# Softmax in halves of eight consecutive blocks, one early transfer of even V rows, and unchained loads of wo

## The chip, the core and the metric

The kernel runs on one core of one Trainium2 chip. The core has a matrix engine (PE, with its weight loads shown as PEld), a vector engine (DVE), a scalar engine (ACT), a general engine (POOL) and a queue engine (SP), each with its own list of instructions and synchronised by semaphores. DMA transfers are issued from SP, ACT and POOL. The metric is the device time of one execution in microseconds (us), lower is better.

## What is computed

Two branches read the same normalised input xn of 2048 tokens by 512: a dilated sliding-window attention with 32 heads of 16 (A), and a gated MLP whose gate mixes all tokens (B). The result is x + A + B.

```python
def _A_ref(x, wqkv, wo):
    H = 32
    Dh = D // H
    W, dil = (8, 2)
    qkv = (lambda x, *d: x.transpose(*d))((x @ wqkv).reshape(B, S, 3, H, Dh), 2, 0, 3, 1, 4)
    q, k, v = (qkv[0], qkv[1], qkv[2])
    idx = pos[:, None] - off[None, :]
    mask = idx >= 0
...
    logits = jnp.einsum('bhsd,bhswd->bhsw', q, kg) * scale
    logits = jnp.where(mask[None, None, :, :], logits, -1000000000.0)
    attn = _softmax(logits, axis=-1)
    o = jnp.einsum('bhsw,bhswd->bhsd', attn, vg)
    return (lambda x, *d: x.transpose(*d))(o, 0, 2, 1, 3).reshape(B, S, D) @ wo

def _B_ref(x, w_in, w_sp, b_sp, w_out):
    z = _gelu(jnp.einsum('bsd,df->bsf', x, w_in))
    z1 = z[..., :Fh].copy()
    z2 = _layernorm(z[..., Fh:], axis=-1)
    g = jnp.einsum('ts,bsf->btf', w_sp, z2) + b_sp[None, :, None]
    return jnp.einsum('bsf,fd->bsd', z1 * g, w_out)
```

Each token attends to itself and to the tokens 2, 4, ... 14 before it.

## The kernel before

The program builds a list of named tasks. A task is one instruction, one DMA, or a short run of matmuls; it belongs to one engine and has the buffers that it reads and writes. From these the program works out what each task must wait for, and an order written out for every engine (ORDERS, L206) says in which sequence each engine works through its tasks. An engine works its list strictly in order: where one task waits, those behind it wait too. Estimates given to the tasks (`est`) make no instruction.

The tokens are in 16 blocks of 128, and the work goes through these stages, each named by the prefix of its tasks:

- **ldx, bnst, norm, xTr / xTd**: x is loaded, normalised and transposed (the first four blocks on PE, the others by transposing DMAs on SP).
- **Q, K, V, z2, z1** on PE: projections by 512 or 448 columns. Their results lie in six banks of PSUM, used as three pairs in turn (0-1, 2-3, 4-5), and ACT empties them: QKe, halo and Ve (L677 to L683, L652), z2g and z1g with the gelu (L818), z2s (L826) with the sum of squares. A pair may be written again once ACT has emptied it. z1_7_0 is the first half of the columns of block 7, z1g7 its gelu.
- **Vw** on SP (L657) writes V to a scratch array in DRAM. **ldV** (L983, issued on ACT) reads it back, so that a partition holds rows two tokens apart: ldV0_k has rows of the even tokens, ldV1_k of the odd ones. The 15 slots of the even rows are read by the even blocks; the odd rows take slots 15 to 22, where the logits stood before, and then slots that the even blocks no longer need.
- **prod, padd** on DVE and **lg** on PE (L694, L698, L707) form the logits of four blocks, **lge** on ACT (L745) copies them to the staging buffer. When all four groups are there, four transposing DMAs **lgT0 to lgT3** on SP (L756) bring tokens to partitions: each holds four consecutive blocks.
- **softmax** (L761 to L796), twice: a tree of three maxima (sm1 to sm3), subtraction (ssub), exponential on ACT (sexp, L783), a tree of three sums (sz1 to sz3), 1/sum as exp(-ln) on ACT (sln L787, srec L789), and the multiplication (sattn, L794). Before, one half is the even blocks and the other the odd blocks, so that the first half needs all four transposes.
- **zn** (L851 on ACT for blocks 12 to 15, L855 on DVE for the others) normalises z2. **T1 to T4** (DVE) are sums of z2 blocks.
- **wT** on SP (L892) loads and transposes w_sp for a pair of output blocks, **S13, S2, S4** (L902 to L908, DVE) sum quarters of it. **P1 to P7** (L930, PE) are seven products of eight matmuls each, which take the place of eight (a Strassen scheme) for each of eight pairs of blocks: (0,2), (4,6), (8,10), (12,14), (15,13), (11,9), (7,5), (3,1). Their banks alternate between 0 to 2 and 3 to 5. fk copies the first product to another bank, S5, S2e, Sc and S3e evacuate (L936, ACT), h adds (L953, DVE), g11, g12, g21 and g22 finish the gate, u multiplies by z1 (L962, L968), and a transposing DMA uT (L972, SP) turns it.
- **pv, pva, pvc** (L1000 to L1008, DVE): attention times V for a pair of blocks, **OTd** its transpose on SP (L1012).
- **out** (PE): four matmuls with wo (L1037) and seven with w_out (L1041), on banks 6 and 7, where **os** (L1032) has put the residual from **ldxr**. **fin** (L1050) evacuates, **st** stores.

wo comes in four loads on POOL's queue (ldwo0 to ldwo3, L1117) that share one channel, so each waits until the one before it has landed; w_out (ldwout) is issued among them. All wait for the last z1 product, whose weights lie in the same memory.

An even V load before the change waits for all V writes and for the four logit transposes; ACT's order has ldV1_7 ahead of z1g3.

Of the kernel before, what the change touches and what calls it, by code (L numbers as in the profile page):

```python
# [14 lines left out]
class Plan:  # L15
# [191 lines left out]
    pe="""  # L207
warm xTr0 fill0 z2_0_0 xTr1 z2_0_1 z2_1_0 xTr2 z2_1_1 xTr3 z2_2_0 z2_2_1 z2_3_0 z2_3_1 Q0_0 K0_0 Q0_1 Q0_2 K0_2
K0_1 K0_3 V2 V1 V0 Q0_3 V7 V3 V4 V6 V5 Q1_0 K1_0 K1_1 Q1_2 Q1_1 Q1_3 K1_3 z2_4_1 K1_2 z2_6_1 z2_6_0 z2_4_0
z2_5_0 z2_5_1 lg0_0 z2_7_1 z2_7_0 V10 V8 V11 V9 K2_0 Q2_0 K2_2 Q2_1 K2_1 Q2_2 K2_3 Q2_3 z2_8_1 z2_8_0 z2_9_0  # L210
z2_9_1 z2_10_1 z2_10_0 z2_11_0 V13 z2_11_1 V14 lg1_0 V12 V15 K3_1 K3_0 Q3_0 K3_2 Q3_1 Q3_3 Q3_2 z2_12_0 z2_12_1
K3_3 z2_13_1 z2_13_0 z2_14_1 z2_15_1 z2_14_0 lg2_0 z2_15_0 z1_0_0 z1_2_1 z1_0_1 z1_2_0 z1_4_0 z1_6_0 z1_4_1
z1_6_1 z1_8_0 z1_8_1 z1_10_1 z1_10_0 z1_12_1 z1_12_0 z1_14_0 z1_14_1 lg3_0 z1_15_1 z1_15_0 z1_13_1 z1_13_0
z1_9_1 z1_9_0 z1_7_1 z1_7_0 z1_11_1 z1_11_0 z1_3_1 z1_3_0 z1_1_0 z1_1_1 z1_5_1 P1_0 z1_5_0 P5_0 P2_0 P1_1 P6_0
P3_0 P7_0 P2_1 P6_1 P5_1 P4_0 P7_1 P3_1 P1_2 P4_1 P2_2 P5_2 P6_2 P1_3 P7_2 P2_3 P4_2 out0_0 P3_2 P6_3 P5_3 P1_4
P3_3 P7_3 out2_0 P5_4 out4_0 P4_3 P6_4 P2_4 P7_4 P1_5 P4_4 P3_4 out6_0 out8_0 P5_5 out10_0 P6_5 P2_5 P1_6 P7_5
out12_0 P4_5 P3_5 P5_6 P6_6 out14_0 P3_6 P7_6 P2_6 P4_6 P1_7 out15_0 P5_7 P6_7 out13_0 out11_0 P2_7 P7_7 P3_7
P4_7 out9_0 out7_0 out5_0 out3_0 out1_0 out1_1
""".split(),
    act="""  # L220
actprime ldw_in2a_1 ldw_in2b_1 ldx3 xTe0 xTe1 z2g0 xTe2 xTe3 z2g1 z2s0 z2g2 z2g3 halo0_0 QKe0_0 QKe0_2 halo0_1
QKe0_1 Ve2 halo0_2 Ve1 Ve0 QKe0_3 Ve3 halo0_3 Ve5 Ve6 Ve4 QKe1_0 halo1_1 z2s1 halo1_0 QKe1_1 Ve7 QKe1_3 halo1_3
z2s2 QKe1_2 z2s3 halo1_2 z2g4 z2g6 z2g5 zm0 z2g7 z2s4 Ve8 Ve11 Ve10 Ve9 halo2_0 z2s5 QKe2_0 z2s6 halo2_2 QKe2_1
lge0 halo2_1 QKe2_2 QKe2_3 halo2_3 z2s7 z2g8 z2g9 z2g10 z2s8 z2g11 Ve14 Ve13 lge1 Ve15 zm1 Ve12 z2s9 QKe3_0
z2s10 QKe3_1 QKe3_2 z2g12 QKe3_3 z2s11 z2g13 z2s12 z2g14 zm2 z2s13 z2g15 z1g0 z2s14 z1g2 z2s15 z1g4 z1g6 lge2
z1g8 z1g10 z1g12 lge3 z1g14 z1g15 z1g13 zn13 z1g9 zn12 z1g7 ldxr0 z1g11 bspf ldV1_7 z1g3 zn14 zn15 z1g1 fk_0
ldV0_0 z1g5 sexp0 fk_1 S5_0 S2e_0 sln0 Sc_0 srec0 S3e_0 S2e_1 S5_1 g11_0 g11_1 S3e_1 g12_0 g21_0 fk_2 Sc_1
ldV0_9 ldxr2 g22_0 g21_1 sexp1 S2e_2 g22_1 S5_2 fk_3 ldV0_11 os0_0 g11_2 S3e_2 g21_2 os2_0 g12_1 Sc_2 ldxr8
S2e_3 g22_2 ldxr6 S5_3 ldxr4 g12_2 fin0_0 g11_3 os4_0 S3e_3 fk_4 sln1 Sc_3 st0_0 ldV0_13 srec1 ldxr10 fin2_0
S2e_4 os6_0 S5_4 fin4_0 ldxr12 os8_0 S3e_4 g22_3 ldV1_6 st2_0 ldV1_4 g12_3 g21_4 Sc_4 g21_3 st4_0 fk_5 fin6_0  # L230
g11_4 os10_0 fin8_0 ldV1_2 os12_0 S2e_5 g22_4 S5_5 ldV1_0 ldxr14 S3e_5 g11_5 st6_0 fin10_0 fk_6 ldxr15 g12_4
fin12_0 st10_0 os14_0 Sc_5 st8_0 ldxr13 ldxr11 g22_5 S5_6 g12_5 g21_5 S2e_6 fin14_0 os15_0 Sc_6 st12_0 S3e_6
st14_0 ldxr9 g11_6 g22_6 g12_6 os13_0 g21_6 fin15_0 fk_7 ldxr7 S5_7 os11_0 fin13_0 fin11_0 S2e_7 os9_0 st11_0
ldxr5 ldxr3 S3e_7 st15_0 os7_0 Sc_7 g11_7 st13_0 ldxr1 g12_7 g22_7 g21_7 fin9_0 os5_0 st9_0 fin7_0 st7_0 os1_1
os3_0 fin5_0 st5_0 os1_0 fin3_0 st3_0 fin1_0 st1_1
""".split(),
    dve="""
zeros steps0 steps1 bnst0 bnag0 norm0 bnst1 bnag1 xTf0 norm1 bnst2 bnag2 bnst3 bnag3 norm2 bnst5 bnag5 norm3
bnst7 bnag7 bnst8 bnst6 bnag6 bnst4 bnag8 norm7 bnag4 bnst9 bnst10 norm5 bnst11 norm6 norm4 bnag11 bnag9 bnag10
prod0_0 prod0_2 prod0_1 norm8 padd0_1 bnst12 bnst13 padd0_2 prod0_3 norm11 bnst15 norm10 bnag15 bnag13 norm9  # L240
bnag12 bnst14 padd0_3 bnag14 prod1_0 prod1_1 zq0 norm13 prod1_2 norm12 zq1 padd1_1 norm14 norm15 padd1_2 prod1_3
prod2_1 padd1_3 prod2_0 zv0 zv1 padd2_1 prod2_2 prod2_3 padd2_2 zq2 smask padd2_3 prod3_1 prod3_0 zv2 prod3_2
padd3_1 zq3 prod3_3 zv3 padd3_2 padd3_3 zn3 zn5 zn0 zn2 S13_1 zn11 zn1 S13_0 zm3 zn6 zn10 zn8 zn9 zn7 T1_0 zn4
T1_1 sm1_0 T3_0 S2_0 S2_1 sm2_0 sm3_0 T3_1 ssub0 T2_1 S4_0 T2_0 T4_1 sz1_0 sz2_0 sz3_0 sm1_1 T4_0 sm2_1 S4_1
sm3_1 ssub1 sattn0 h_0 pv0 pv2 pva2048_0 pva1024_0 pvc0 S13_2 S2_2 u_0 S4_2 sz1_1 h_1 pv4 sz2_1 S13_3 pv6 S2_3
pva2048_1 sz3_1 S4_3 u_4 h_2 pva1024_1 pvc1 pv8 pv10 S13_4 pva2048_2 u_8 h_3 pva1024_2 S2_4 pvc2 S4_4 sattn1
pv12 pv14 pva2048_3 pva1024_3 S13_5 pvc3 u_12 S2_5 pv13 h_4 pv15 S13_6 S4_5 pva2048_4 pva1024_4 S2_6 pvc4 pv9
S4_6 pv11 h_5 pva2048_5 u_11 pva1024_5 u_15 pvc5 pv5 S13_7 h_6 pv7 S2_7 pva2048_6 u_7 pva1024_6 pvc6 S4_7 pv3
pv1 pva2048_7 pva1024_7 pvc7 h_7 u_3 u_1 fin1_1
""".split(),  # L250
# [4 lines left out]
    sp="""
ldx0 ldx1 ldw_in2a_0 ldw_in2b_0 ldx2 ldx4 ldx5 ldx8 ldx6 ldx7 ldq ldk ldx9 ldx10 ldx11 ldwv xTd7 xTd5 xTd4 ldx15
xTd6 ldx12 ldx14 Vw1 Vw2 ldx13 Vw0 xTd8 Vw3 Vw7 xTd11 xTd10 Vw4 Vw6 Vw5 xTd9 xTd12 xTd13 xTd14 xTd15 Vw9 Vw10
Vw11 Vw8 wT1_1 ldw_in1 wT0_0 wT0_1 Vw15 Vw12 Vw14 wT1_0 Vw13 lgT0 lgT1 lgT3 lgT2 wT2_0 wT2_1 wT3_0 wT3_1 OTd0
uT_0 wT4_0 uT_2 wT4_1 OTd1 uT_4 uT_6 wT5_0 uT_8 uT_10 OTd2 wT5_1 wT6_0 wT6_1 uT_12 OTd3 uT_14 OTd4 wT7_0 wT7_1
uT_15 uT_13 uT_11 uT_9 OTd5 uT_7 OTd6 uT_5 OTd7 uT_3 uT_1 st1_0  # L260
# [926 lines left out]
```

## Time and profile before

| | us |
|---|---|
| median of 3 runs (lowest, highest) | 228.18 (227.88, 228.59) |
| the profiled execution: its own time | 228.81 |
| its span, first to last instruction | 227.1 |
| busy PE / DVE / ACT / POOL | 221.8 / 203.8 / 147.8 / 35.3 |
| the first and the last product P on PE start | 100.15 / 211.2 |
| the last matmul ends | 224.8 |

The page's chain that ended last gives 85% of the span to PE, by line:

```profile
PE 85%; DMA 6%; SPq 3%; ACT 2%; DVE 2%; issue 1%; ACTq 0%; DVEq 0%
PE ps L930 33%; PE ps L807 15%; PE ps L669 12%; PE ps L1041 11%; PE ps L646 6%; PE ps L1037 6%; DMA arena<-in_B_w_sp_dram 3%; DMA arena<-in_A_x_dram 2%; SPq L756 2%; DMA arena<-arena 1%; ACT arena L818 1%; PE ps L707 1%; ACT arena L851 1%; DVE fpool L595 1%; DVE arena L902 1%
```

The V loads in the table of DMA issues (line, count, size, us from issue to landing):

```profile
arena<-vscr ACTq DMA_DIRECT2D x6, 256.0 KB, 4.2
arena<-vscr ACTq DMA_DIRECT2D x1, 1152.0 KB, 7.7
arena<-vscr ACTq DMA_DIRECT2D x1, 1024.0 KB, 6.0
```

How to read it: a row of the timeline has the start, the length, the engine, the line, the operation and the count of instructions that follow each other, and in brackets the idle time before with what ended it. Matmul lengths are modelled and longer than the distance from one to the next, so PE is timed by starts. A span's share of idle time costs only on the engine that sets the end.

### The profile page before, as it was taken

How to read it: one execution, taken by the hardware profiler on the slowest of the kernel's cores; microseconds unless marked ns; L12 is line 12 of the kernel's file. 1: busy time of each engine (PE TensorE's matmuls, PEld its weight loads, DVE VectorE, ACT ScalarE, POOL GpSimd, SP SyncE). 2: the span in 40 equal slices, each digit the busy share in tenths (PEclk: the TensorE clock that was granted, in tenths of full speed). 3: DMA queues.
4: the chain of work that ended last, by engine and by line, in shares of the span. 5: the costliest groups of instructions: out<-in, count | busy, mean ns of one | idle time of the engine just before them, and what ended most of it. 6: DMA issues, size and time to landing. Idle time of an engine off the chain costs nothing.

```text
span 227.1 us, 3070 instructions
## 1 busy us (share of the span) xinstructions
PE 221.8 (98%) x1130; PEld 115.6 (51%) x1142; DVE 203.8 (90%) x208; ACT 147.8 (65%) x258; POOL 35.3 (16%) x40
## 2 busy tenths in 40 slices
...
PEclk9999999999999999999999999999999999999999
DMA  6969605148982000959749995887996495936562
GB/s 191 298 157 186 190 0 146 22 92 214 225 219 61 0 0 4 160 146 309 124 140 217 266 202 120 171 210 141 280 169 152 115 203 140 213 67 151 128 124 69
DMA packets 84767, 34.18 MB, mean 151 GB/s; under 512 B 69280, under 2 KB 84400, under 8 KB 84752
## 3 DMA queue, kind: packets, MB, share of 16 engines
...
## 4 chain that ended last, share of the span: by engine, by line
PE 85%; DMA 6%; SPq 3%; ACT 2%; DVE 2%; issue 1%; ACTq 0%; DVEq 0%
PE ps L930 33%; PE ps L807 15%; PE ps L669 12%; PE ps L1041 11%; PE ps L646 6%; PE ps L1037 6%; DMA arena<-in_B_w_sp_dram 3%; DMA arena<-in_A_x_dram 2%; SPq L756 2%; DMA arena<-arena 1%; ACT arena L818 1%; PE ps L707 1%; ACT arena L851 1%; DVE fpool L595 1%; DVE arena L902 1%
## 5 line engine op out<-in xcount | busy, mean ns | idle before, releaser
L930 PE MATMUL ps<-arena 128*128 128x448 bf16 x448 | 86.7, 352 | 0.8 <-ACT arena L818 0.4
L930 PEld LDWEIGHTS ps<-arena 128*128 128x128 bf16 x448 | 43.6, 98 | 42.9 <-ACT arena L818 0.8
L807 PE MATMUL ps<-arena 128*128 128x448 bf16 x256 | 51.3, 355 | 0.2 <-DVE arena L629 0.2
L807 PEld LDWEIGHTS ps<-arena 128*128 128x128 bf16 x256 | 30.5, 121 | 19.1 <-issue 1.3
L1000 DVE TENSOR_TENSOR arena<-arena 128x4096 bf16<-128x4096 bf16 x16 | 36.2, 2285 | 0.3
L936 ACT ACTIVATE arena<-ps 128x448 bf16<-128x448 f32 x32 | 17.3, 540 | 29.4 <-PE ps L930 25.3
L694 DVE TENSOR_TENSOR arena<-arena 128x4096 bf16<-128x4096 bf16 x16 | 36.0, 2283 | 0.2 <-PE ps L707 0.2
L818 ACT ACTIVATE arena<-ps 128x896 bf16<-128x896 f32 x32 | 28.9, 916 | 6.2 <-PE ps L807 6.2
L669 PE MATMUL ps<-arena 128*128 128x512 bf16 x126 | 28.5, 379 | 0.1
L1004 DVE TENSOR_TENSOR arena<-arena 128x4096 bf16<-128x4096 bf16 (+1 forms) x16 | 28.1, 1753 | 0.2
L698 DVE TENSOR_TENSOR arena<-arena 128x4096 bf16<-128x4096 bf16 x12 | 27.4, 2282 | 0.0
L1041 PE MATMUL ps<-arena 128*128 128x512 bf16 (+2 forms) x117 | 26.9, 366 | 0.1
L600 POOL TENSOR_TENSOR fpool<-fpool 128x1 f32<-128x1 f32 x16 | 19.2, 1207 | 20.0 <-DVE fpool L598 19.9
L669 PEld LDWEIGHTS ps<-arena 128*128 128x128 bf16 x128 | 14.5, 113 | 13.1
L677 ACT ACTIVATE arena<-ps 128x1024 bf16<-128x1024 f32 x16 | 16.2, 1025 | 4.0 <-PE ps L669 4.0
L1050 ACT ACTIVATE arena<-ps 128x512 bf16<-128x512 f32 (+1 forms) x16 | 9.4, 589 | 13.4 <-PE ps L1041 13.4
L1041 PEld LDWEIGHTS ps<-arena 128*128 128x128 bf16 x119 | 11.4, 98 | 12.8
L1037 PE MATMUL ps<-arena 128*128 128x512 bf16 (+2 forms) x63 | 15.5, 365 | 0.3
L826 ACT ACTIVATE arena<-arena 128x896 bf16<-128x896 bf16 x16 | 15.2, 950 | 0.0
L646 PE MATMUL ps<-arena 128*128 128x512 bf16 x61 | 14.3, 379 | 0.2
L595 DVE BATCH_NORM_STATS2 fpool<-arena 128x6 f32<-128x512 bf16 x16 | 10.6, 676 | 3.2 <-DMA arena<-in_A_x_dram 3.1
L958 ACT ACTIVATE arena<-arena,fpool 128x448 bf16<-128x448 bf16 x16 | 10.4, 662 | 4.1 <-DVE arena L953 2.4
...
## 6 DMA issues: line engine op xcount, KB each, us to landing
...
arena<-vscr ACTq DMA_DIRECT2D x6, 256.0 KB, 4.2
arena<-vscr ACTq DMA_DIRECT2D x1, 1152.0 KB, 7.7
arena<-vscr ACTq DMA_DIRECT2D x1, 1024.0 KB, 6.0
```

The source lines that it names most:

```text
L600: T("pool", lambda g: g.tensor_tensor(Fv("rstd", 1, b), Fv("mv", 1, 2 * b + 1), Fv("mhalf", 1), ALU.pow), reads=[("mv", b), "mhalf"], writ ...
L646: last = t.matmul(bank(k + i), AC(off["xnT"] + dc * S + 128 * (b + i), [[1, 128]]), AC(off["wv_raw"] + 512 * dc, [[1, 512]]), start=(dc == ...
L669: last = t.matmul(bank(k + which), AC(off["wqk"] + 1024 * dc + col0, [[4, 128]]), AC(off["xnT"] + dc * S + 512 * j, [[1, 512]]), start=(dc ...
L694: T("dve", lambda v: v.tensor_tensor(pbv, qb, kb, ALU.mult), reads=[("QT", c, j), ("KT", c, j), ("KTpad", c, j)], writes=[("pb", s_)], est ...
L698: T("dve", lambda v: v.tensor_tensor(A("pb", 4096, 4096 * a), A("pb", 4096, 4096 * a), A("pb", 4096, 4096 * b), ALU.add), reads=[("pb", b) ...
L807: last = t.matmul(bank(k + hf, HF), AC(off["xnT"] + dc * S + t0, [[ts, 128]]), AC(off["w_in"] + 1792 * dc + c0, [[1, HF]]), start=(dc == 0 ...
L818: T("act", lambda a: a.activation(A(nm, FH, FH * b).rearrange("p (t n) -> p t n", t=2), PC(512 * k, [[512, 2], [1, HF]]), ACTF.Gelu_apprx_ ...
L930: last = t.matmul(bank(k, HF), AC(lo + 128 * s, [[1, 128]]), mov(s), start=(first and s == 0), stop=(s == 7), skip_group_check=True)
L1000: T("dve", (lambda iv, tv, av: lambda v: v.tensor_tensor(tv, iv, av, ALU.mult))(iv, tv, av), reads=[("attn", pairs[i][b]) for b in blks] + ...
L1004: T("dve", (lambda n: lambda v: v.tensor_tensor(AC(off["Vs"], [[4096, 2], [1, n]]), AC(off["Vs"], [[4096, 2], [1, n]]), AC(off["Vs"] + n, ...
L1037: t.matmul(po, AC(off["OT"] + 512 * os_ + 128 * cc, [[1, 128]]), AC(off["wo"] + 512 * cc + c0, [[1, n]]), start=False, stop=False, skip_gr ...
L1041: last = t.matmul(po, AC(off["uT"] + FH * us + 128 * fc, [[1, 128]]), AC(off["w_out"] + 512 * fc + c0, [[1, n]]), start=False, stop=(fc == ...
```

## The change

Softmax works on blocks 0 to 7 and 8 to 15 in place of even and odd blocks. All 15 slots of even V rows come in one transfer, which waits for the V writes alone and is created ahead of the logit transposes; these now wait for it. The loads of wo have a channel each. Two estimates differ. All five orders are new; the main stages keep their sequence, and inside them tasks change places. The core of the diff:

```diff
-                T("pe", mm, reads=[("pb", s_), "mlog"], writes=[("ps", 6), ("ps", 7)], est=570.0,
+                T("pe", mm, reads=[("pb", s_), "mlog"], writes=[("ps", 6), ("ps", 7)], est=760.0,
...
+        def ld_v(par, k0, n):
+            s0 = k0 + 8 * par
+            src = bass.AP(tensor=vscr.tensor, offset=vscr.offset + (par + 2 * k0 + 2) * 512,
+                          ap=[[16 * 512, 128], [1024, n], [1, 512]])
+            dma("act", lambda e: e.dma_start(AC(off["Ve"] + 512 * s0, [[512, n], [1, 512]]), src), 128 * 512 * 2 * n,
+                ("Ve", s0), reads=[("vscr", i) for i in range(-1, NB)] + ([("lgTd", i) for i in range(4)] if par else []), writes=[("Ve", s0 + i) for i in range(n)],
+                name="ldV%d_%d" % (par, k0), prio=LOW)
...
-                    128 * 1024 * 2, ("lgT", n), reads=["stage"] + [("lgs", j) for j in range(NJ)],
+                    128 * 1024 * 2, ("lgT", n), reads=["stage"] + [("lgs", j) for j in range(NJ)] + [("Ve", 0)],
...
-        def softmax(par):
+        def softmax(half):
...
-            a0 = off["attn"] + 256 * par
-            ks = [("attn", b) for b in range(par, NB, 2)]
-            nm = "%d" % par
+            a0 = off["attn"] + 2048 * half
+            ks = [("attn", b) for b in range(8 * half, 8 * half + 8)]
+            nm = "%d" % half
...
-                T("dve", lambda v: v.tensor_tensor(AC(off["Za"], [[128, 8], [1, 128]]), AC(a0, [[512, 8], [1, 128]]),
-                                                   AC(a0 + 128, [[512, 8], [1, 128]]), op),
+                T("dve", lambda v: v.tensor_tensor(AC(off["Za"], [[128, 8], [1, 128]]), AC(a0, [[256, 8], [1, 128]]),
+                                                   AC(a0 + 128, [[256, 8], [1, 128]]), op),
...
-            dv = AC(a0, [[512, 8], [32, 8], [1, 32]])
+            dv = AC(a0, [[256, 8], [32, 8], [1, 32]])
...
-            ev = AC(a0, [[512, 8], [1, 256]])
+            ev = AC(a0, [[256, 8], [1, 256]])
...
-                      reads=[("m2", j), ("rstd2", j)], writes=[("z2", b, 0), ("z2", b, 1)], est=c_act(FH), name="zn%d" % b)
+                      reads=[("m2", j), ("rstd2", j)], writes=[("z2", b, 0), ("z2", b, 1)], est=c_act(FH) + 210.0, name="zn%d" % b)
...
             if j == NJ - 1:
+                ld_v(0, 0, 15)
                 lg_transposes()
...
-                128 * 512 * 2, "wo", writes=[("wo", c)], name="ldwo%d" % c)
+                128 * 512 * 2, ("wo", c), writes=[("wo", c)], name="ldwo%d" % c)
...
-        vloads = {0: [(0, 0, 9)], 1: [(0, 9, 2)], 2: [(0, 11, 2)], 3: [(0, 13, 2)], 4: [(1, 7, 8), (1, 6, 1)],
+        vloads = {4: [(1, 7, 8), (1, 6, 1)],
                   5: [(1, 4, 2)], 6: [(1, 2, 2)], 7: [(1, 0, 2)]}
```

The new orders, where the prediction follows them (the ones before stand in the kernel above):

```diff
     pe="""
...
+z1_8_1 z1_8_0 z1_12_0 z1_4_1 z1_12_1 z1_14_0 z1_10_1 z1_10_0 z1_13_0 z1_13_1 lg3_0 z1_15_1 z1_15_0 z1_14_1
+z1_7_1 z1_9_1 z1_7_0 z1_9_0 z1_11_0 z1_11_1 z1_3_1 z1_3_0 z1_1_1 z1_1_0 z1_5_0 z1_5_1 P1_0 P1_1 P2_0 P5_0 P6_0
+P6_1 P5_1 P7_0 P2_1 P3_0 P4_0 P1_2 P7_1 P3_1 P4_1 P2_2 P1_3 P5_2 P6_2 P3_2 P7_2 P2_3 P4_2 P5_3 out0_0 P6_3
+out2_0 P7_3 P3_3 P4_3 P1_4 P5_4 P6_4 out4_0 P2_4 P7_4 out6_0 P1_5 P4_4 P2_5 P5_5 P3_4 P6_5 P1_6 P7_5 P2_6 out8_0
...
     act="""
...
+QKe3_0 z2s10 QKe3_1 z2s11 QKe3_2 QKe3_3 z2g12 z2s12 z2g13 z2g14 z2g15 z2s13 ldV0_0 z1g0 z2s14 z1g2 z1g6 z2s15
+lge2 z1g8 z1g4 z1g12 zm2 z1g10 z1g13 lge3 z1g15 zn13 z1g14 zn12 z1g9 bspf z1g7 zn15 z1g11 ldxr4 z1g3 z1g1 zn14
+fk_0 z1g5 sexp0 fk_1 S2e_0 sln0 srec0 S5_0 S3e_0 ldxr2 Sc_0 g11_0 g12_0 S2e_1 g21_0 g22_0 S5_1 g11_1 fk_2 S3e_1
+g21_1 sexp1 Sc_1 g12_1 ldxr0 S5_2 fk_3 g22_1 S2e_2 os0_0 ldxr6 S3e_2 Sc_2 g21_2 sln1 srec1 os2_0 S2e_3 g11_2
+fin0_0 S5_3 st0_0 g12_2 S3e_3 g22_2 Sc_3 ldV1_7 ldxr8 g11_3 os4_0 g21_3 fin2_0 ldxr10 fk_4 S5_4 S2e_4 os6_0
...
     dve="""
...
+padd3_1 zq3 prod3_2 prod3_3 zv3 smask padd3_2 padd3_3 zn4 zn6 S13_1 zn0 zn7 zm3 zn1 S13_0 S2_0 zn11 zn5 zn2 S4_0
+zn8 T1_1 zn10 S2_1 T1_0 sm1_0 zn9 sm2_0 T3_0 sm3_0 ssub0 T3_1 T2_0 T2_1 S4_1 sz1_0 sz2_0 sm1_1 sz3_0 sm2_1 sm3_1
+T4_0 ssub1 T4_1 sattn0 pv2 h_0 pv0 pva2048_0 u_0 pva1024_0 S13_2 S2_2 S4_2 h_1 sz1_1 pvc0 sz2_1 pv4 pv6 S13_3
+sz3_1 S2_3 pva2048_1 u_4 pva1024_1 sattn1 pvc1 h_2 S4_3 pv8 pv10 S13_4 u_8 S2_4 pva2048_2 pva1024_2 h_3 pvc2
...
     pool="""
...
+rstd11 rstd9 Vzero rstd8 rstd13 rstd15 rstd12 rstd14 ldbsp zr0 zr1 zr2 zr3 ldwo2 ldwo3 ldwo1 ldwo0 ldwout
...
     sp="""
...
+xTd13 ldw_in1 wT0_0 wT1_0 wT1_1 Vw14 Vw12 Vw13 wT0_1 Vw15 lgT0 lgT1 lgT2 lgT3 wT2_0 wT3_0 wT2_1 uT_2 uT_0 wT3_1
+OTd0 wT4_1 wT4_0 OTd1 uT_6 uT_4 wT5_0 wT5_1 wT6_0 wT6_1 OTd2 OTd3 uT_8 uT_14 uT_10 wT7_0 OTd4 uT_12 wT7_1 uT_15
...
```

83 lines of the change are left out of this document (30 added, 53 removed).

## The prediction

> **What bounds the kernel now.** I read the page's first two parts for the engine that sets the end.
>
> ```profile
> PE 221.8 (98%) x1130; PEld 115.6 (51%) x1142; DVE 203.8 (90%) x208; ACT 147.8 (65%) x258; POOL 35.3 (16%) x40
> ...
> PEclk9999999999999999999999999999999999999999
> DMA  6969605148982000959749995887996495936562
> ```
>
> PE is busy 98% of the span at the full granted clock. That share alone could hide slow matmuls, so I looked at the pitch. The last line of this piece of the chain of waits (start, length, what) gives it: 9.08 / 48 = 0.189 us for each matmul with 448 columns. ```profile
> 118.29 6.38 DMA arena<-in_B_w_sp_dram
> ...
> 124.76 1.24 DVE arena L902
> ...
> 126.05 9.25 PE ps L930 x48
> ...
> 137.67 9.08 PE ps L930 x48
> ```
>
> A product P is eight of these, 1.51 us; an output block is eleven of 512 columns at 0.216 (`147.62 1.51 PE ps L1041 x7`), 2.38 us. From 11 us to 224.8 us nearly every start follows the last at this pitch. The zeros in the DMA row (70 to 85 us) are a stretch with nothing in flight. So PE's own work is the floor, and what can be won is PE's waiting. The waits of PE name the places, the timeline sizes them.
>
> ```profile
> PE ps L930 <- ACT arena L818: 0.4, 1, 0.4
> PE ps L930 <- issue: 0.2, 1, 0.2
> PE ps L930 <- DVE arena L902: 0.2, 1, 0.2
> ```
>
> Here the timeline for PE alone, 88 to 104 and 117 to 136 us (start, length, line, count):
>
> ```profile
> 88.35 11.57 PE L807 MATMUL ps<-arena 128*128 128x448 bf16 x60
> 100.15 1.67 PE L930 MATMUL ps<-arena 128*128 128x448 bf16 x8 [0.23 <-issue]
> 101.66 0.92 PE L807 MATMUL ps<-arena 128*128 128x448 bf16 x4
> 102.95 1.31 PE L930 MATMUL ps<-arena 128*128 128x448 bf16 x6 [0.37 <-ACT arena L818]
> ```
>
> ```profile
> 116.77 9.05 PE L930 MATMUL ps<-arena 128*128 128x448 bf16 x47
> 126.05 9.25 PE L930 MATMUL ps<-arena 128*128 128x448 bf16 x48 [0.22 <-DVE arena L902]
> ```
>
> By pitch, 88.35 + 60 x 0.1892 = 99.7, but P1_0 starts at 100.15: 0.4 lost. 101.66 + 4 x 0.1892 = 102.42, P5_0 starts at 102.95: 0.53 lost. 116.77 + 47 x 0.1892 = 125.66, P5_2 starts at 126.05: 0.39 lost. Together **1.32 us**, which is all that PE waits after 11 us. The timeline of all engines around 98 us says what was late.
>
> ```profile
> 98.31 0.69 DVE L768 TENSOR_TENSOR arena<-arena 128x1024 bf16<-128x1024 bf16 x1 [2.31 <-DMA arena<-arena]
> 98.49 0.60 ACTq L983 DMA_DIRECT2D arena<-vscr  x1
> ...
> 99.13 0.92 ACT L818 ACTIVATE arena<-ps 128x896 bf16<-128x896 f32 x1 [1.94 <-PE ps L807]
> ```
>
> ACT stands idle 1.94 us before the gelu z1g3. The row blames PE, but z1_3_0 ended at 97.5. What ACT stood at is the V load of L983 just ahead of it in its order (ldV1_7), which waits for the last of the four logit transposes; DVE's softmax (L768) waits for the same landing, 2.31 us. z1g3 ends at 100.05 and P1_0 needs its bank (100.15); z1g1 ends at 102.90 and P5_0 needs its bank (102.95). The third loss is the first three lines of the chain above: weights transposed after P4_0 (wT2_1), summed by S13_2, awaited by P5_2.
>
> **The change part by part.** PE's list has the same tasks, so PE's work is unchanged. The estimates raised at L711 and L853 go to no instruction: 0.
>
> *Even V rows in one transfer.* Four transfers (9, 2, 2 and 2 rows) become one of 15, 1920 KB, issued on ACT behind z2s13 (about 76.5 us), and it no longer waits for the logit transposes. ldV1_7 moves to about 147 us, 50 us after what it waits for. So the two bank waits of 0.4 and 0.53 lose their cause: **-0.93**. Issues on ACT took 0.33 to 0.72 us (L983) and ACT has 6.2 us of waits on PE at L818, so the issue costs 0, or 0.7 of ACT's time without that cover. It waits for all sixteen V writes on SP's queue; the last was issued at 67.3 and such writes land in 1.7 to 2.8 us, so it stalls nothing behind it (z1g0). New is that the logit transposes on SP wait for it; behind them stands wT2_0, which waits for P2_0 (105.0) anyway. No row has 1920 KB: below, it cannot beat the 7.7 us of 1152 KB; above, at the rate of w_in's 896 KB in 7.6 us beside two transposes, 16.3. It lands between 84.2 and 92.8; I take 12.8 (1152 KB scaled, the nearest row), 89.3. The transposes start at 90.6 anyway: lg3 stands one z1 half later on PE (87.80 + 0.76) and lge3 behind z1g13 on ACT (89.7 + 0.92). At the upper end the first half's logits land at 92.8 + 6.0 (as lge3 to lgT1 now, 89.5 to 95.5) = 98.8 instead of 96.6, and T2_1 ends 1.5 us later, 106.1, still ahead of P6_0 at 106.5. So 0, and at worst the last 0.4 of slack.
>
> *Softmax by halves.* The same instructions and sizes with another stride: 0. The first half needs lgT0 and lgT1 alone. DVE reaches it at 97.4: padd3_3 ends at 86.4 + 0.43 (zn3 now goes before it), then from start to start ten zn at 0.43, two S13 at 1.13, two S2 and S4_0 at 0.61, two T1 at 1.0. So the 2.31 us wait is gone, and T2_1 ends 7.2 us on, 104.6. DVE pays some back: sexp0 stands behind fk_0 and z1g5 (P1_0's end 102.0 + 0.2 + 0.5 + 0.9 + load 1.28 + 1.91 = 106.8), and sz1_0 waits 1.5 us for it. DVE finishes 10 us before PE now (last u_1 at 215.4), so this is worth nothing by itself. The other half is needed sooner: sattn1 before pv8 (142 us) instead of pv15 (170).
>
> *ln and exp together.* sln0 and srec0, with a table load each, now stand in one block ahead of S5_0.
>
> ```profile
> 109.78 1.28 ACT L787 ACT_TABLE_LOAD   x1
> 111.07 0.42 ACT L787 ACTIVATE fpool<-fpool 128x256 f32<-128x256 f32 x1
> 111.39 0.53 ACT L936 ACTIVATE arena<-ps 128x448 bf16<-128x448 f32 x1
> 111.94 1.28 ACT L789 ACT_TABLE_LOAD   x1
> 113.23 0.42 ACT L789 ACTIVATE arena<-fpool 128x256 bf16<-128x256 f32 x1
> ```
>
> Walk: z sum ready 106.8 + 0.69 + 0.43 + 0.68 (sm1_1) + 0.42, by overlap 108.9; + 1.28 + 0.42 + 1.28 + 0.42 = 112.4, S5_0 to 112.9; P3_0 needs it at 114.1: 1.2 of slack. The second block stands behind g21_2, so it starts with P4_2's end (135.3): 0.2 + 0.62 + 3.4 + os2_0 0.59 = 140.1; out2 comes at 135.3 + 1.51 + 2.38 + 1.51 = 140.7: slack 0.6. A switch dearer than its load would eat both; the rows show none: the gelu before sexp0 ends at 104.16, the load starts at 104.18 and sexp0 at 105.47 (rival C). The Trainium skill, "ScalarE: Activation LUTs", section "What ACT_TABLE_LOAD costs", does add a drain of about 1.38 us to the load's 1.28 for every switch; by it the sum would be some 5 us worse, and the trace so far contradicts it.
>
> *wo unchained.* POOL's 13.1 us of waits between the four loads go. They are needed at out0, now at 136.8; the last was issued at 119.1 and they land in 4.0 to 6.9 (L1117), so by 126.0 even chained: 0, covered by 10.8 us.
>
> *The orders.* I walked PE from P1_0 at 100.5 (99.7 + one z1 half) in the new order at 1.51 and 2.38, and ACT and DVE with their rows (evacuation 0.54 to 0.63, starting 0.2 behind the product; pv and padd 2.28). P4_0 now ends at 117.1, not 118.1; SP puts wT3_0 (released at 114.1, issue 3.2) ahead of wT2_1, issued at 117.4, landing +6.4 = 123.8, S13_2 done 125.1, and P5_2 comes at 126.2 because P1_3 goes first: the third wait, **-0.39**, is gone with 1.1 to spare. Thin places: P1_2 at 117.1 needs g11_0, done 116.9; P3_1, P7_1 and P4_1 (118.6 to 121.7) have 0.35 to 0.4; P7_3 and P3_3 0.5 (they need h_2, thus sattn1, at 142). Before 76 us the walk finds no bank later than 0.2 before its use. Bounds of what the thin places cost: 0 (each margin holds), or 1.2 (ACT 1.3 late at P1_2, the slack that the second half of the ln block hides elsewhere). I take 0.25, near the lower end, since all durations repeat within 3%.
>
> **Sum**: -0.93 - 0.39 + 0.25 = -1.07. Span 227.1 becomes 226.0. The profiled run took 228.81, 1.7 around its span; the runs shown have a median of 228.18, so I forecast 228.18 - 1.07 = **227.1**.
>
> **Rivals.**
> *A, no change.* The handovers from ACT are late by more than their margin. For: P1_2's is 0.2, and ACT works through one unbroken list from 115.8 to 121.2 there, so one lateness runs on. Against: a stall of PE reopens the margins behind it, so they don't add up. Giving back 0.5 to 1.2: 227.5 to 228.2.
>
> *B, slower: SP's queue ahead of out8.* wT6_1 now stands before OTd2, OTd3 and uT_8 and waits for P4_4, which ends at 162.9 in the new order. Transposes of w_sp hold SP 1.3 to 6.8 us (median 2.6), then 1.3 for each of OTd2 and OTd3, then uT_8 lands in 2.9 to 5.0. Median: 162.9 + 2.6 + 2.6 + 3.1 = 171.2, out8 comes at 173.5: no stall. With 6.8 and 5.0: 177.3, a stall of 3.8, and 227.1 + 3.8 = 230.9. It makes the kernel slower by over 0.3% once uT_8 lands after 173.5 + 1.07 + 0.7 = 175.3. For: the wT6 loads now meet V loads, wT6_1 took 3.5 and 7.8 before. Against: the even V rows are out of that stretch. Typical case: 229.2.
>
> *C, a table switch holds ACT longer than its record.* Say one more load's length, 1.28. Three switches ahead of S5_0 make it 3.8 late, past its slack of 1.2, so P3_0 waits 2.6; two ahead of os2_0 make it 2.6 late, so out2 waits 2.0: 227.1 + 4.6 = 231.7. Against: the rows at 104 and 110 us. The page of the Trainium skill named above states such a cost.
>
> *D, the change doesn't do what it says*: the V load lands after lge3, the softmax waits as before. PE keeps only the loss of 0.4 at T2: 227.5, counted with A.
>
> **How the numbers follow.** Forecast 0.55, A with D 0.22, B 0.21, C 0.02. About 0.3% (0.7 us) is what a measurement of this kernel can tell from no change: faster means below 227.5. So faster 0.55, same 0.22, slower 0.23. The likeliest case has 226.6 (no thin place costs, and 0.3 of noise) to 227.5; all PE waits gone is the hard floor, about 226.9. The range for 8 in 10 reaches down to 226.5 and up through A and most of B to 229.4.
>
> **What would show it.** Right: no idle ACT before z1g3, P1_0 within 0.1 of the last z1; no DVE wait at L768; PE waits on L930 under 0.3 in all; DMA busy where the zeros were. Wrong: PE L930 waiting for ACT L936 (A), PE L1041 or L1037 waiting for a transposed u (B), over 1.4 us between ACT's work and the ln behind a load (C), the logit transposes starting well behind lge3 (D).

## The result and the profile after

| | before | after |
|---|---|---|
| median of 14 runs each, taken side by side (lowest, highest), us | 228.86 (227.88, 230.63) | 227.21 (226.8, 231.7) |
| span of the profiled execution, us | 227.1 | 225.4 |
| PE's waits after 11 us, us | 1.32 | 0 |
| first product P on PE starts, us | 100.15 | 100.14 |
| last matmul ends, us | 224.77 | 223.07 |

The ratio of after to before is 0.9933, with a 95% interval of 0.9908 to 0.9959: the changed kernel is faster by 0.7%. The run of 231.7 us, at a mean granted clock of 0.993, is not in the ratio. The forecast was 227.1 us.

The page of the changed kernel, busy engines and the DMA row:

```profile
PE 221.6 (98%) x1142; PEld 116.0 (51%) x1142; DVE 203.6 (90%) x208; ACT 148.6 (66%) x258; POOL 36.3 (16%) x40
...
DMA  6955705026994460946955928998699975198872
```

PE does the same work. Before, the DMA row has three zeros, the slices from 74 to 91 us; two of them are gone, since the early V load runs there, and the one from 85 to 90 us stays. The chain that ended last, by engine, and PE's waits (line, what it waited for, us in total, times, longest):

```profile
PE 98%; DVE 0%; issue 0%
```

```profile
PE ps L567 <- DVE fpool L494: 1.3, 1, 1.3
PE ps L815 <- issue: 0.2, 1, 0.2
```

Before, that chain had 13% of waits for DMA, SP, ACT and DVE in it; now 98% of it is PE, released by PE itself. The first wait is that of the first matmul and stood there before too; the product line (L930 before, L938 now) is in the list no more. The timeline of PE around the first two of the old waits, and then around the third:

```profile
88.73 11.58 PE L815 MATMUL ps<-arena 128*128 128x448 bf16 x60
100.14 4.14 PE L938 MATMUL ps<-arena 128*128 128x448 bf16 x21
```

```profile
115.65 20.97 PE L938 MATMUL ps<-arena 128*128 128x448 bf16 x110
```

A row begins anew where PE pauses or its line changes. 88.73 + 60 x 0.1892 = 100.08, and P1_0 starts at 100.14; and 110 matmuls follow each other in one row from 115.65 to out0 at 136.46, across the place at 126 us where the old timeline broke. ACT and the softmax at 98 us, where ACT stood idle for 1.94 us and DVE for 2.31:

```profile
97.03 2.71 ACT L826 ACTIVATE arena<-ps 128x896 bf16<-128x896 f32 x3
...
103.22 1.28 ACT L791 ACT_TABLE_LOAD   x1
104.52 1.91 ACT L791 ACTIVATE arena<-arena 128x2048 bf16<-128x2048 bf16 x1
```

```profile
97.83 0.69 DVE L776 TENSOR_TENSOR arena<-arena 128x1024 bf16<-128x1024 bf16 x1
```

The gelus z1g11, z1g3 and z1g1 follow each other without a pause, and the softmax (L776) has no bracket, so no wait. Last, the w_sp transposes whose issue runs between 116 and 119.5 us (line, count, median us from issue to landing), first before, then after:

```profile
arena<-in_B_w_sp_dram SPq DMA_TRANSPOSE x1, 6.4
```

```profile
arena<-in_B_w_sp_dram SPq DMA_TRANSPOSE x2, 4.2
```

wT2_1, which P5_2 waited for, lands in 4.26 us in place of 6.38. That line turned out to be the one to follow, though in the changed kernel S13_2 no longer waits for it. It landed at 121.24, and DVE came to S13_2 two us later:

```profile
122.12 1.22 DVE L1004 TENSOR_TENSOR arena<-arena 128x2048 bf16<-128x2048 bf16 x1
123.26 1.22 DVE L910 TENSOR_TENSOR arena<-arena 128x2048 bf16<-128x2048 bf16 x1
```

S13_2 (L910) ends at 124.48, and P5_2 starts at 125.87.

**Accounting.** The span is 1.7 us shorter. 1.32 of it are the three waits. The rest, 0.4, is the start: z2_3_1 ends at 13.62 us and not at 14.04. Nothing here shows that to be the change's. I took the end of the last matmul less all PE waits after 25 us in eleven of the profiled kernels (those without half-speed matmuls): it lies between 222.9 and 224.6, with 223.45 before and 223.07 after, and it follows when x and w_qkv arrive. Kernels with the old orders at the start and kernels with the new ones both spread over most of that range.

### The profile page after: what moved, and what is told of

It reads as the page before. It is cut to its first block, busy times and chain, and to the rows that moved or that the text cites. A ratio compares the mean times of both kernels' runs of the same rounds, so it can differ in the third digit from the quotient of the medians.

```text
span 225.4 us, 3078 instructions
## 1 busy us (share of the span) xinstructions
PE 221.6 (98%) x1142; PEld 116.0 (51%) x1142; DVE 203.6 (90%) x208; ACT 148.6 (66%) x258; POOL 36.3 (16%) x40
## 4 chain that ended last, share of the span: by engine, by line
PE 98%; DVE 0%; issue 0%
PE ps L938 38%; PE ps L815 22%; PE ps L669 12%; PE ps L1041 11%; PE ps L646 6%; PE ps L1037 6%; PE ps L567 2%; PE ps L707 1%; PE ps L619 0%; DVE arena L1049 0%; DVE arena L493 0%; DVE fpool L494 0%
## 5 line engine op out<-in xcount | busy, mean ns | idle before, releaser
L938 PE MATMUL ps<-arena 128*128 128x448 bf16 x448 | 86.7, 353 | 0.0
L938 PEld LDWEIGHTS ps<-arena 128*128 128x128 bf16 x448 | 43.8, 98 | 41.4 <-issue 0.2
L669 PE MATMUL ps<-arena 128*128 128x512 bf16 x128 | 29.1, 379 | 0.0
L1041 PE MATMUL ps<-arena 128*128 128x512 bf16 (+2 forms) x119 | 27.0, 367 | 0.0
L1041 PEld LDWEIGHTS ps<-arena 128*128 128x128 bf16 x119 | 11.4, 98 | 12.8
L1037 PE MATMUL ps<-arena 128*128 128x512 bf16 (+2 forms) x68 | 16.6, 367 | 0.0
L944 ACT ACTIVATE arena<-ps,fpool 128x448 bf16<-128x448 f32 x16 | 10.0, 630 | 7.6 <-PE ps L938 6.2
L646 PE MATMUL ps<-arena 128*128 128x512 bf16 x64 | 15.0, 380 | 0.0
L851 POOL TENSOR_TENSOR fpool<-fpool 128x4 f32<-128x4 f32 x4 | 10.3, 2572 | 22.9 <-DVE fpool L848 22.9
```

What stands on the lines that cost most here:

```text
L646: last = t.matmul(bank(k + i), AC(off["xnT"] + dc * S + 128 * (b + i), [[1, 128]]), AC(off["wv_raw"] + 512 * dc, [[1, 512]]), start=(dc == ...
L669: last = t.matmul(bank(k + which), AC(off["wqk"] + 1024 * dc + col0, [[4, 128]]), AC(off["xnT"] + dc * S + 512 * j, [[1, 512]]), start=(dc ...
L938: last = t.matmul(bank(k, HF), AC(lo + 128 * s, [[1, 128]]), mov(s), start=(first and s == 0), stop=(s == 7), skip_group_check=True)
L944: T("act", lambda a: a.activation(dst, bank(k, HF), ACTF.Identity, **kw), reads=[("ps", k), "bspf"], writes=[key], est=est, name="%s_%d" % ...
L1037: t.matmul(po, AC(off["OT"] + 512 * os_ + 128 * cc, [[1, 128]]), AC(off["wo"] + 512 * cc + c0, [[1, n]]), start=False, stop=False, skip_gr ...
L1041: last = t.matmul(po, AC(off["uT"] + FH * us + 128 * fc, [[1, 128]]), AC(off["w_out"] + 512 * fc + c0, [[1, n]]), start=False, stop=(fc == ...
```

## Experiments

The table has the gaps of PE in the places that matter, measured from start to start less the pitch, in us. "one run" is a single time without an interval. The kernel before had a median of 228.86 us beside the changed one and of 229.16 to 229.64 beside the others.

| kernel | P1_0 | P5_0 | P6_0 | P5_2 | out8 | span | ratio to before |
|---|---|---|---|---|---|---|---|
| before | 0.39 | 0.54 | 0 | 0.39 | 0 | 227.1 | 1 |
| e1 before, odd V later | 0 | 0 | 0.42 | 0.70 | 0 | 226.6 | 0.9998 [0.9979, 1.0018] |
| e2 e1 and swapped order | 0 | 0 | 0 | 3.55 | 0 | 231.8 | 1.0177 [1.0154, 1.0201] |
| e3 before, swapped order | 0.67 | 0.54 | 0 | 3.52 | 0 | 232.0 | 1.0186 [1.0168, 1.0205] |
| e4 before, early even V | 0.48 | 0.49 | 0 | 0.09 | 0 | 226.6 | 0.9957 [0.9940, 0.9975] |
| e9 e3 and wo unchained | 0.47 | 0.54 | 0 | 0 | 0 | 226.2 | 0.9951 [0.9926, 0.9976] |
| e10 before, wo unchained | 0.34 | 0.54 | 0 | 0 | 0 | 226.2 | 0.9952 [0.9924, 0.9979] |
| e11 before with four parts | 0 | 0 | 0 | 0 | 0 | 226.9 | 0.9919 [0.9887, 0.9950] |
| after | 0 | 0 | 0 | 0 | 0 | 225.4 | 0.9933 [0.9908, 0.9959] |
| e5 after, odd V back | 0 | 0 | 0 | 0 | 0 | 225.9 | 227.64 us, one run |
| e6 after, even and odd softmax | 0 | 0 | 0 | 0 | 0 | 225.5 | 0.9927 [0.9896, 0.9957] |
| e7 after, wo chained | 0 | 0 | 0 | 1.91 | 0 | 229.1 | 230.93 us, one run |
| e8 after, uT_8 later | 0 | 0 | 0 | 0 | 3.95 | 232.8 | 1.0137 [1.0088, 1.0186] |
| e12 after, even V back | 0 | 0 | 0 | 0 | 0 | 225.9 | 0.9940 [0.9913, 0.9968] |

**e1: the odd V load alone.** Does ldV1_7, ahead of z1g3, make the two bank waits?

```diff
-z1g11 bspf ldV1_7 z1g3
+z1g11 bspf z1g3
...
-st0_0 ldV0_13 srec1
+st0_0 ldV0_13 ldV1_7 srec1
```

> The kernel before with one name moved: ldV1_7 goes from ahead of z1g3 to behind ldV0_13 (about 147 us) in ACT's order. Theory (ACT stood at this load, and the two bank waits of 0.4 and 0.53 us follow from it): no idle ACT before z1g3, P1_0 within 0.1 us of z1_5_1's end, no wait at P5_0; the wait at P5_2 stays at 0.3 to 0.5, since its chain moves along with PE. PE's waits 0.4 in all in place of 1.3, span shorter by 0.9. Rival (the softmax or the early transfer brought it): PE's waits stay at 1.0 to 1.3 and the time stays.

Both waits went, as the theory said, but the time stayed (0.9998), since PE ran into two others. The first, in PE's timeline of e1 (the bracket has the idle time and what ended it):

```profile
101.73 4.70 PE L930 MATMUL ps<-arena 128*128 128x448 bf16 x24
106.68 3.58 PE L930 MATMUL ps<-arena 128*128 128x448 bf16 x18 [0.26 <-DVE arena L879]
```

101.73 + 24 x 0.1892 = 106.27, and P6_0 starts at 106.68 because T2_0 on DVE ends at 106.63: DVE still waits for the last logit transpose, as before, and it was PE's lateness that had hidden it. The second is P5_2's, which grew from 0.39 to 0.70: PE came there 0.8 us earlier, S13_2 only 0.5. So a wait taken away is worth no more than the margin behind it.

**e2 and e3: the order of SP and PE around the third wait**, with and without e1.

```diff
-lgT2 wT2_0 wT2_1 wT3_0 wT3_1
+lgT2 wT2_0 wT3_0 wT2_1 wT3_1
...
-P2_2 P5_2 P6_2 P1_3 P7_2 P2_3 P4_2 out0_0 P3_2 P6_3
+P2_2 P1_3 P5_2 P6_2 P3_2 P7_2 P2_3 P4_2 out0_0 P6_3
...
-S2e_2 g22_1 S5_2 fk_3
+S5_2 g22_1 S2e_2 fk_3
```

> The kernel before with the move of ldV1_7 and the swap around P5_2: wT3_0 ahead of wT2_1 on SP, P1_3 ahead of P5_2 and P3_2 behind P6_2 on PE, S5_2 ahead of S2e_2 on ACT. Parity softmax, split V loads and chained wo stay. Theory: all three waits gone, PE's waits 0 to 0.2, span shorter by 1.2 to 1.3, as much as the change gave after 11 us. Rival (the change's named parts count): at least 0.5 us of waits stays.

> The kernel before with the swap around P5_2 alone. Theory: the wait of 0.39 at P5_2 goes, the waits at P1_0 and P5_0 stay at 0.9 together; span shorter by 0.4. Rival (the wait at P5_2 came from crowded DMA, not from the order): wT2_1 lands as late against its need as before, 0.3 or more of waiting at P5_2 or at P1_3.

The swap is part of the changed kernel's orders and was expected to take the third wait away. It made it 3.5 us long, in both kernels, and the time 1.8% longer. In the DMA issues of e3 from 113 to 124 us stands why (KB each, median us to landing):

```profile
arena<-in_B_w_out_dram POOLq DMA_DIRECT2D x1, 896.0 KB, 9.4
arena<-in_A_wo_dram POOLq DMA_DIRECT2D x2, 128.0 KB, 6.9
...
arena<-in_B_w_sp_dram SPq DMA_TRANSPOSE x2, 10.3
```

wT3_0 (113.88 to 123.52) and wT2_1 run side by side with w_out and two loads of wo, and all five take 1.2 to 1.7 times as long as in the kernel before (9.38 for w_out, 6.15 there). wT2_1 held SP for 5.66 us and landed 11.03 us after its issue, at 129.44. And the wait cost more than its length, as the windows of PE in e3 show (PE busy and matmuls, granted clock, DMA share, GB/s):

```profile
122.00:127.00 5.00, 5.00 (x28) 1.00 1.13 285
127.00:132.00 5.00, 1.65 (x9) 0.99 1.09 189
132.00:135.00 3.00, 3.00 (x9) 0.50 0.40 77
```

28 matmuls fall in the 5 us before the wait; from 132 to 135 us the granted clock is 0.50 and 9 fall in 3 us, 0.374 us from one to the next in place of 0.189. That gives away another 1.69 us behind a wait of 3.52; it sets in 1.2 us after PE has gone on (130.82). The Trainium skill, "TensorE: Matmul & The Clock Gate", section "What's actually happening", has the array fall to half its clock after an idle window of about 3.4 us, and come back after as long a busy one. The trace agrees: half speed after 3.52 us, for some 3.4 us, and in e7 none after 1.91. No run has a wait between these two. In e2, where P1_0 came 1.1 us later than in e1 (100.58 and 99.46), T2 was in time for P6_0; the rest went as in e3.

**e4: the early even V load alone**, with the transposes waiting for it and ldV1_7 still ahead of z1g3.

```diff
+                ld_v(0, 0, 15)
                 lg_transposes()
...
-        vloads = {0: [(0, 0, 9)], 1: [(0, 9, 2)], 2: [(0, 11, 2)], 3: [(0, 13, 2)], 4: [(1, 7, 8), (1, 6, 1)],
+        vloads = {4: [(1, 7, 8), (1, 6, 1)],
```

> The kernel before with the even V rows in one transfer behind z2s13, the logit transposes waiting for it, and all else as before; ldV1_7 stays ahead of z1g3. Theory: the early transfer is worth nothing by itself: it lands before lge3, ACT still idles 1.5 to 2 us before z1g3, the waits at P1_0 and P5_0 stay at 0.8 to 1.0; only P5_2's wait can shrink, by 0 to 0.4, since w_sp's transposes meet fewer V loads. Span shorter by 0 to 0.4. Rival (taking the V rows off the crowded stretch is the gain): shorter by 0.9 or more.

The bank waits stayed, but the third wait all but went (0.09). Without 1152 KB of V beside it ldwo0 landed in 4.20 us and not in 6.88, the chain of wo and w_out behind it ran some 2 us ahead, and wT2_1 had fewer bytes beside it (6.08 us in place of 6.38, issued 0.2 earlier). The time is shorter than these waits say: they shrank by 0.26 us, and the ratio of 0.9957 stands for 1.0, at least 0.6 by its interval (more at e10).

**e5 and e6: two parts of the change undone.** e5 puts ldV1_7 back ahead of z1g3, e6 makes the softmax's halves the even and the odd blocks again, each in the changed kernel with all else kept.

```diff
-z1g11 ldxr4 z1g3 z1g1
+z1g11 ldxr4 ldV1_7 z1g3 z1g1
```

```diff
-            a0 = off["attn"] + 2048 * half
-            ks = [("attn", b) for b in range(8 * half, 8 * half + 8)]
+            a0 = off["attn"] + 256 * half
+            ks = [("attn", b) for b in range(half, NB, 2)]
```

> The changed kernel with ldV1_7 put back ahead of z1g3 on ACT. Theory: z1g3 starts only when the last logit transpose has landed and the load is issued (98.8 + 0.6 = 99.4 in place of 97.8) and ends at 100.3; P1_0 waits 0.2 to 0.4 us for its bank. The wait at P5_0 doesn't come back, since P1_1 and P2_0 now stand ahead of it. Span longer by 0.2 to 0.4. Rival (ACT's place for this load doesn't matter): P1_0 starts as now and the span stays.

> The changed kernel with the softmax by even and odd blocks again, all orders as they are. Theory: DVE's first maximum waits for the last transpose, 0.9 to 1.1 us later than now; T2_1 ends at 105.7, still ahead of P6_0 (106.2); PE waits 0 to 0.1 and the time is the same within 0.1%. Rival (the halves bring part of the gain): PE waits 0.5 us or more at P6_0, P3_0 or P1_2, and the time is longer by as much.

e5 missed: no wait came back. z1_5_1 ends at 100.65 and P1_0 starts at 100.65. ACT does stand 0.93 us ahead of z1g3 there, but with both halves of z1_5 ahead of P1_0 and two products between P1_0 and P5_0 the banks are wanted later (P5_0 at 105.2, not 102.4). So the bank waits are covered twice in the changed kernel: by ACT's order and by PE's. e6 has the same time as the changed kernel: the halves by themselves bring nothing. DVE waits 0.49 us there for the last transpose, not 2.31 as before, since the new order gives it other work until shortly before, and T2 stays in time.

**e7: wo chained again**, in the changed kernel, with w_out last on POOL.

```diff
-                128 * 512 * 2, ("wo", c), writes=[("wo", c)], name="ldwo%d" % c)
+                128 * 512 * 2, "wo", writes=[("wo", c)], name="ldwo%d" % c)
...
-ldwo2 ldwo3 ldwo1 ldwo0 ldwout
+ldwo0 ldwo1 ldwo2 ldwo3 ldwout
```

> The changed kernel with the four loads of wo on one channel again, in POOL's old order with w_out last. Theory: POOL waits some 13 us between them, w_out lands by 126, out0 comes at 136.5: nothing on PE, span the same within 0.1 us. Rival: PE waits before out0, or wT2_0 lands sooner and something moves ahead.

The theory, which had taken this part to be worth nothing, fell: 230.93 us. The piece of the chain that ended last and PE's longest wait in e7:

```profile
118.44 9.42 DMA arena<-in_B_w_sp_dram
```

```profile
PE ps L938 <- DVE arena L910: 1.7, 1, 1.7
```

ldwo3 and w_out go out at 116.9 and 117.6 us and land at 122.9 and 126.0. wT2_1, issued beside them at 118.44, holds SP for 7.33 us and lands after 9.42, where the changed kernel needs 4.26. With the early V load and the new orders all in place, P5_2 waits 1.91 us, and two products behind it wait 0.3 together. The span is 3.7 us longer, but not all of that is this wait: by the last matmul's end less all waits, 1.5 of it is a later start.

**e8: uT_8 one place later on SP**, to price rival B.

```diff
-OTd3 uT_8 uT_14 uT_10
+OTd3 uT_14 uT_8 uT_10
```

> The changed kernel with uT_14 ahead of uT_8 on SP, the mechanism of the prediction's rival B pushed by one transpose. uT_8 lands now at 172.8, out8 starts at 173.2. Theory (that margin of 0.4 is real and beyond it PE pays one for one): uT_8 is issued at 170.2 to 170.9, lands at 174.2 to 174.9, out8 waits 1.0 to 1.7 us, and the span is longer by the same. Rival (something else gives way, or the lost time is made up behind it): longer by under 0.5.

out8 waited 3.95 us in the profiled execution, not 1.0 to 1.7. uT_8 was issued at 171.63 (168.86 in the changed kernel) and landed after 6.14 us in place of 3.97. It ran beside ldV1_4, issued at 172.65, and beside stores and other transposes; which of them slowed it isn't separated. The profiled execution was the longest of six, 234.61 us; by the ratios the other runs lose 1.0137 / 0.9933, about 2% of the changed kernel's time. The mechanism of rival B is real, and dearer than this expectation had it; the changed kernel had escaped it by 0.37 us (uT_8 landed at 172.83, out8 started at 173.20).

**e9 and e10: unchained wo in the kernel before**, with the swapped order of e3 and alone.

```diff
-                128 * 512 * 2, "wo", writes=[("wo", c)], name="ldwo%d" % c)
+                128 * 512 * 2, ("wo", c), writes=[("wo", c)], name="ldwo%d" % c)
...
-ldwo0 ldwo1 ldwo2 ldwout ldwo3
+ldwo2 ldwo3 ldwo1 ldwo0 ldwout
```

> The kernel before with the swapped order of e3 (wT3_0 ahead of wT2_1) and the loads of wo unchained. Theory, a crowded queue: the wait of 3.5 us came because the w_sp transposes ran beside the chained loads of wo and w_out; unchained, these have landed by about 111 us, so wT3_0 lands 4 to 5.5 us after its issue at 114 (9.64 in e3), wT2_1 issues in 2 to 3 us (5.7) and lands by 124, S13_2 ends by 125.5 and P5_2, due at 127.2, doesn't wait; only the two bank waits of 0.9 stay: span 226.5 to 227, ratio 0.997 to 1.000. Rival, the order itself: wT2_1 stands behind wT3_0 on SP and can't land in time; the wait stays near 3.5 us with the slow matmuls behind it: 233, ratio about 1.018.

> The kernel before with the loads of wo unchained and nothing else. Theory: wT2_1 meets fewer bytes and lands 4.3 to 5.2 us after its issue, not 6.38, so P5_2's wait of 0.39 goes and the bank waits of 0.9 stay: span 226.5 to 226.8, ratio 0.997 to 0.999. Rival, as the prediction had it: unchaining is worth 0; wT2_1 lands 6 to 6.7 us after its issue and the third wait stays at 0.3 to 0.5.

The same order that lost 3.5 us in e3 loses nothing in e9: wo and w_out have landed by 113.7, wT2_1 is through 4.72 us after its issue, and S13_2 ends at 124.82, 1.9 us ahead of P5_2. In e10 the third wait goes with no order changed on PE or SP; its timeline of PE across the old gap at 125.7:

```profile
114.81 16.43 PE L930 MATMUL ps<-arena 128*128 128x448 bf16 x86
```

86 matmuls in one row, S13_2 done at 124.85, P5_2 at 125.22. So the crowd on the queue was the cause, the order was not. What unchaining does is not to make wo earlier for out0, which never wanted it, but to move its bytes and w_out's from 114 to 124 us into 102 to 114, where wT2_0 and the V loads stand beside them. wT2_0 pays (it lands 9.5 us after its issue in e10, 5.3 before), and no wait of PE came of it.

Both ratios are better than was expected (0.997 to 1.000 for e9, 0.997 to 0.999 for e10), and better than the waits explain. In the profiled executions PE's waits shrank by 0.31 us in e9 and 0.44 in e10, while 0.9951 and 0.9952 stand for 1.1 us each, with at least 0.5 by their intervals. With e4 these are three kernels without the third wait, or nearly, that gain 1.0 to 1.1 us; e1 keeps that wait and gains nothing. It would fit if the third wait is longer in most executions of the kernel before than the 0.39 of the profiled one, but there is no trace of a second execution to show it. So the places of the waits are shown, and the share of each part in the time stays open.

**e11 and e12: what is enough, and what is spare.** e11 builds the gain from the kernel before with four parts: the early even V load (e4), ldV1_7 later (e1), wo unchained (e10), and the swapped order (e3); DVE's T3_0, S2_0 and S2_1 go ahead of sm1_0 so that T2 isn't late. e12 takes the early V load out of the changed kernel and has four even loads again.

```diff
-T1_1 sm1_0 T3_0 S2_0 S2_1 sm2_0
+T1_1 T3_0 S2_0 S2_1 sm1_0 sm2_0
```

```diff
-z2s13 ldV0_0 z1g0
+z2s13 z1g0
...
-fk_0 z1g5
+fk_0 ldV0_0 z1g5
...
-fk_2 S3e_1
+fk_2 ldV0_9 S3e_1
```

> The kernel before with four parts alone: the early even V transfer, ldV1_7 later, wo unchained, and the swapped order of e3, with T3_0, S2_0 and S2_1 ahead of sm1_0 on DVE so that T2 is not late. Softmax stays by even and odd blocks and the other orders stay. Theory: these parts hold the whole gain; PE waits after 20 us 0.3 at most in all, span 225.4 to 226.1, ratio 0.991 to 0.996, the same as the changed kernel within its interval. Rival: the rest of the new orders is needed too; a wait of 0.4 or more stays at P6_0 (T2) or P5_2, span 226.4 or more, ratio 0.997 or more.

> The changed kernel with the even V rows back in four loads behind the transposes (9 rows behind fk_0, then 2, 2 and 2). Theory, that the crowd of wo and w_out decides: the 9 rows land by 112, wT3_0 and wT2_1 then run nearly alone and land 4 to 5.5 us after their issue, P5_2 keeps 0.3 or more of margin, no wait: span 225.3 to 225.9, ratio 0.991 to 0.996. Rival, that the V loads decide: wT2_0 and with it wT3_0 and wT2_1 come late, P5_2 waits 0.4 to 1.5: span 226 to 227.

e11 has the whole gain: 0.9919, the same as the changed kernel within the intervals, and no wait on the product line. Its span is longer than the theory had it because of the start alone, as its waits of PE show:

```profile
PE ps L669 <- DMA arena<-in_A_wqkv_dram: 0.8, 2, 0.5
PE ps L815 <- DVE arena L629: 0.7, 1, 0.7
```

All its waits lie before 22 us, where no part differs from the kernel before. e12 keeps the gain too, though the 9 even rows now need 11.90 us beside wo and w_out and wT2_1 6.11: S13_2 ends at 125.12, 1.2 us ahead of P5_2. With wo unchained and the new orders, the early V load is spare.

No kernel of these beat the changed one clear of the noise, and with PE's work as it is none could by much: its PE doesn't wait after 11 us. What is left is the start and 2.3 us behind the last matmul.

## Why the prediction was right, and where it was not

*The floor and the three waits.* PE's pitch as the floor, and 1.32 us of waits as all there was to win: right. All three went and nothing came in their place. The zeros of the DMA row stand at 74 to 91 us, not 70 to 85; no term hangs on that.

*The bank waits, -0.93.* The mechanism is shown: e1 moves ldV1_7 alone and both waits go. What the prediction didn't see is that the new order of PE covers them a second time (e5), and that in the old orders the next wait, at T2, would have taken 0.42 back (e1).

*The third wait, -0.39.* The amount was right and the reason given was not enough. It was put down to the orders: wT3_0 ahead of wT2_1, P1_3 ahead of P5_2, with wT2_1's landing left at the old 6.4. e3 shows the same order losing 3.5 us where the queue is crowded. In the changed kernel the margin is 1.4 us (S13_2 ends at 124.48, P5_2 starts at 125.87), where 1.1 was forecast, and DVE sets it, not wT2_1: by these figures the order would have held with a landing of 6.4 us too. It doesn't hold with the 9.42 of chained loads (e7).

*The step that failed: wo unchained, 0.* It was covered, the prediction said, by the 10.8 us until out0. That looked only at who waits for wo, not at who runs beside it. e10 gives that part the third wait by itself, 0.39, and e7 shows that the changed kernel without it waits 1.91 us at the same place. The early V load, put at 0 too, took 0.30 off the third wait in the old kernel (e4) and nothing in the new (e12). The two errors and the order's undue credit cancel in the sum, which is luck. The text ahead of the prediction also has every wo load waiting for the last z1 product; ldwo2 was issued at 85.9 us in the changed kernel.

*The early V load's time.* It was put at 84.2 to 92.8 us, with 89.3 taken. It landed at 84.03, just under the lower end: it was issued at 74.88 and not 76.5, and its 9.15 us lie between the bounds of 7.7 and 16.3, below the 12.8 taken. The transposes started at 90.14 behind lge3, as said, not behind the load; rival D is out.

*The softmax and the ln block.* sm1_0 at 97.83 (97.4 predicted), T2_1 done at 104.75 (104.6), S5_0 at 112.34 (112.9), out2 0.62 behind os2_0 (0.6). Rival C is out: the load of 1.28 us ends at 104.50 and sexp0 starts at 104.52. The drain that "ScalarE: Activation LUTs" of the Trainium skill adds in "What ACT_TABLE_LOAD costs" isn't in this trace.

*The thin places, +0.25.* They cost nothing. P1_2 came 0.25 us after g11_0 (0.2 predicted), P7_3 0.51 after S2e_3 and P3_3 0.58 after S5_3 (0.5). Rival A is out.

*Rival B.* Right in place and sign, and its point was near: a margin of 0.37 us where the median case had 2.3. Its worst case, 230.9, is about what e8 cost: 228.18 x 1.0137 = 231.3.

*The sum.* -1.07 predicted; -1.32 from the waits and -0.39 from a start that differs from one execution to the next. The allowance of 0.25 and the start are all of the difference between the profiled spans. That the median came within 0.1 us of the forecast (227.21 and 227.1) is in part luck. The forecast started from 228.18, and the kernel before had 228.86 beside the changed one; and the ratio stands for 1.5 us gained, with 0.9 to 2.1 by its interval, not 1.07. The two differences nearly cancel.
